# Moving 24 weight stores from ScalarE's queue to GpSimd's in an attention and MLP kernel

## The chip, the cores and the metric

The kernel runs on one core of one Trainium2 chip. The metric is the device time of one execution in microseconds (us). Unless another unit is given, all times below are microseconds, and times inside an execution count from the start of the profiled span.

## The reference, cut to what matters

Two kinds of layer alternate over an activation `x` of 2048 rows by 640 columns, in float32: attention over a dilated sliding window (32 heads of 20, a window of 8 keys at a distance of 2), then an MLP (640 to 1536 to 640, GELU), then both once more with the same weights. Each is preceded by a layer norm and added to `x`.

```
x = x + A(layernorm(x), wqkv, wo)          # q, k, v = x @ wqkv; window softmax; @ wo
x = x + B(layernorm(x), w1, b1, w2, b2)    # layernorm(x); gelu(x @ w1 + b1) @ w2 + b2
x = x + A(layernorm(x), wqkv, wo)
x = x + B(layernorm(x), w1, b1, w2, b2)
```

## The kernel before, in words

**Precision.** Every float32 matmul is made of three float16 ones. An operand is split into a high half and a low half; high by high, high by low and low by high are added up in PSUM. Weights are scaled by 64 first.

**Units.** The 2048 rows are cut into four units of 512 rows (4 tiles of 128). One layer of one unit is a block `n` or `b` from 0 to 7; blocks 0 to 3 are the first layer, 4 to 7 the second. A block goes through: a layer norm; the qkv product on TensorE (L522), drained from PSUM by ScalarE (`ev`, L537) and spilled to memory by a DMA that ScalarE issues (L543); windows of q, k and v fetched back by SyncE's queue (L562); the window attention on VectorE (L601 to L639); the output product (L667); a second layer norm; the MLP, whose first product (L721) goes through GELU on ScalarE (L727, L730) and a subtraction on VectorE (L732) into the second product (L742). Three PSUM tiles (`ps`) serve L522, L667 and L721 in turn, so TensorE stops when ScalarE or VectorE leaves three of them undrained.

**The MLP weights.** `w1` and `w2` don't stay on chip. They are split once, early on, and written to memory as float16 pairs (`mw`); each pass of the MLP reads them back (L714, 216 loads over the whole kernel). The splitting runs in 24 steps (12 slices of 128 hidden columns, for `w1` and `w2` each), named `prep_m`:

1. SyncE's queue loads 320 KB of float32 weights into a staging slot (L382; 8 steps at first, blocks of `wo` among them, through four slots in `yT`, the rest through four slots `sa` in the tile `act`).
2. ScalarE writes the high half into a slot of `c1` or `c2` (L356).
3. VectorE writes the low half beside it (L357), which frees the staging slot.
4. A DMA stores the pair (320 KB) to `mw` (L397). Its landing frees the slot of `c1` or `c2`; there are three of each.

The same six slots take the weights that the MLP reads back later. The first product of the MLP waits until all low halves are written (`split_done`).

**The order of work.** Nothing is scheduled on the chip: each engine runs its own program in order, and an instruction whose semaphore hasn't come holds up all that stand behind it on that engine. The order is written when the kernel is built, by the class `Plan`. Each operation has an engine, a duration, a priority and what it needs; `Plan.run` plays the engines forward with these durations, always takes the operation that can begin first (among those that can, the one of the lowest priority number), and sorts all operations by the start that comes out. For a DMA it also keeps `hw`, until when the last DMA's issue lasts (on whichever engine), and `bus`, until when the queued bytes take; a DMA marked `lazy`, as the stores to `mw` are, isn't started earlier than 3 us before the bus is free. So a duration in the plan doesn't slow the chip, but it decides the order in which every engine's program is written.

**GpSimd.** Its other work is a few constants at the start, eight small operations for the first two layer norms (L449) and 30 operations that raise a variance to the power of -0.5 (L471). ScalarE makes the variance (L468) and waits for the result (L475).

The step that changes, and the helper that gives a DMA its cost in the plan:

Of the kernel before, what the change touches and what calls it, by code (L numbers as in the profile page):

```python
# [40 lines left out]
AHEAD = 1.5  # L41

ENDS = 2

HURRY = {3: 0.9, 7: 0.9, 11: 0.9}

# [157 lines left out]
def sliding_dilated_then_mlp_kernel(  # L204
# [18 lines left out]
    nc = tc.nc  # L223
# [11 lines left out]
    plan = Plan(SLOTS)  # L235
# [29 lines left out]
    def tile_of(pool, key):  # L265
        return T[pool][plan.slot[pool, key]]
# [20 lines left out]
    mw = [[dram.tile([P, 2, D], HT, name=f"mw{i}{f}") for f in range(NF)] for i in range(2)]  # L287
# [15 lines left out]

    def dma(kb, prio, emit, need=(), give=(), use=(), by="sp"):
        lazy = give[0][0] in ("x", "sq", "st", "c1", "c2", "zero", "mw") or give[0] in ("b1", "b2")
        plan.add(by, 0.1 if by == "act" else 0.38, prio, emit, need, give, use, move=kb / 330.0, lazy=lazy)

    def dma_transpose(prio, emit, need=(), give=(), use=()):
        plan.add("sp", 1.45, prio, emit, need, give, use, move=1.4)
# [16 lines left out]
    def identity():  # L326
# [4 lines left out]
    pool(0.3, -850, mask_index, give=["mi"])  # L331
    dve(32, -850, mask_value, need=["mi"], give=["mask"])
    dma(6, 40, lambda: nc.sync.dma_start(b1, bass.AP(tensor=B_b1.tensor, offset=B_b1.offset, ap=[[1, P], [P, NF]])),
        give=["b1"])
    dma(320, 41, lambda: nc.sync.dma_start(b2, bass.AP(tensor=B_b2.tensor, offset=B_b2.offset, ap=[[0, P], [1, D]])),
        give=["b2"])

    zk = ("sa", "zero")
    pool(0.3, -840, lambda: nc.gpsimd.memset(tile_of(*zk)[:HALO, :GC], 0.0), give=["zeros"], use=[zk])
    for la in range(2):  # L340
        for par in range(2):
            def clear(la=la, par=par):
                to = spill[la][par]
                z = tile_of(*zk)[:HALO, :GC]
                nc.sync.dma_start(bass.AP(tensor=to.tensor, offset=to.offset, ap=[[GC, HALO], [ROWS * GC, 3 * NG], [1, GC]]),
                                  z[:, None, :].to_broadcast([HALO, 3 * NG, GC]))

            dma(54, -490 + 300 * la + 100 * par, clear, need=["zeros"], give=[("zero", la, par)], use=[zk])
# [27 lines left out]
    def prep_rows(name, prio, src, hi, lo, use=()):  # L376
        key = (through[name], name)

        def load():
            st = tile_of(*key)  # L380
            w = src()
            nc.sync.dma_start(st.rearrange("p (k c) -> p k c", k=w.shape[1]) if len(w.shape) == 3 else st, w)  # L382

        dma(P * D * 4 / 1e3, prio, load, need=[("ev", 0, M - 1, 0)], give=[("st", name)], use=[key])
        a, v = split(hi, lo, lambda: tile_of(*key))
        act(D, prio, a, need=[("st", name)], give=[("hi", name)], use=[key, *use])
        dve(D, LOP[key[0]], v, need=[("hi", name)], give=[("lo", name)], use=[key, *use])
# [4 lines left out]
    def prep_m(f, i, prio):  # L392
        ck = (f"c{i + 1}", ("prep", f))
        src = (lambda: B_w2[f * P:(f + 1) * P]) if i else (
            lambda: B_w1.rearrange("(k p) c -> p k c", p=P)[:, :, f * P:(f + 1) * P])
        prep_rows(("m", f, i), prio, src, lambda: tile_of(*ck)[:, 0], lambda: tile_of(*ck)[:, 1], [ck])
        dma(328, prio - 5, lambda: nc.scalar.dma_start(mw[i][f], tile_of(*ck)),  # L397
            need=[("lo", ("m", f, i))], give=[("mw", f, i)], use=[ck], by="act")

    def turn(prio, t, name, key, yk):  # L400

# [280 lines left out]
    def mlp(at, b, t0, t1):  # L682
# [12 lines left out]
        tiles = range(t0, t1)  # L695
        ends = ENDS if at == len(PARTS) - 1 else 1
        closing = []
# [113 lines left out]
    for f in range(NF):  # L811
        for i in range(2):
            prep_m(f, i, 10 + f)
# [49 lines left out]
```

## Time and profile before

| | us |
|---|---|
| median of 3 runs (lowest, highest) | 1173.69 (1172.49, 1174.92) |
| the profiled execution, own time | 1173.78 |
| its span, first to last instruction | 1171.8 |
| TensorE busy | 1156.6 |
| VectorE busy | 1017.9 |
| ScalarE busy | 513.5 |
| GpSimd busy | 50.6 |

The span is what the trace covers; the profiled execution's own time is 1.98 us longer. Busy time of TensorE is the time in which at least one matmul is in flight. Its mean granted clock is 0.998 of full speed.

### The profile page before, as it was taken

To read this page: it belongs to the slowest core of one execution; us is meant where nothing else is said; L and a number is where in the kernel's file an instruction comes from. 1 tells how busy PE (TensorE), PEld (TensorE's weight loads), DVE (VectorE), ACT (ScalarE), POOL (GpSimd) and SP (SyncE) were. 2 spreads that over 40 slices of the span, in tenths; PEclk is the share of its full clock that TensorE was granted. 3 is DMA by queue.
4 is the path that set the end of the run, shared out by engine and by line. 5 is a ranking of instruction groups with operands and counts; after the bars stand their busy time and mean duration, and the time that the engine had idled before them with its cause. 6 is when DMAs were issued, how large, how long until landed. Compare 5 with 4: busy or idle time off the path is not lost.

```text
span 1171.8 us, 17254 instructions
## 1 busy us (share of the span) xinstructions
PE 1156.6 (99%) x6902; PEld 626.4 (53%) x6902; DVE 1017.9 (87%) x989; ACT 513.5 (44%) x925; POOL 50.6 (4%) x46
## 2 busy tenths in 40 slices
PE   8999999999999999999999999999999999999998
PEld 5444445577655455444655465545555655565554
DVE  8898999999899999999999999999999999821211
ACT  5385345446355336723446334373423453343211
POOL 1010002000000001100101000000100000000000
PEclk9999999999999999999999999999999999999999
DMA  9989999887987475775675666568655774545432
GB/s 304 331 294 247 270 329 284 241 270 247 219 219 213 154 206 145 206 191 173 169 208 176 175 194 191 179 170 189 180 191 180 208 196 134 177 102 135 146 102 79
DMA packets 219773, 235.01 MB, mean 201 GB/s; under 512 B 129884, under 2 KB 170412, under 8 KB 219692
## 3 DMA queue, kind: packets, MB, share of 16 engines
q1 hardware_dynamic: 190636, 194.57, 59.6%
q10 hardware_dynamic: 29056, 39.33, 10.0%
q8 instruction: 54, 0.88, 0.3%
q14 instruction: 27, 0.22, 0.1%
HBM read 158.93 MB, written 44.78 MB: 174 GB/s over the span
## 4 chain that ended last, share of the span: by engine, by line
PE 84%; DMA 7%; DVE 6%; issue 2%; ACT 1%; SPq 0%; POOL 0%; ACTq 0%; DVEq 0%
PE ps L522 29%; PE ps L721 22%; PE acc L742 22%; PE ps L667 11%; DMA yT<-hl 3%; DMA act<-in_B_w_dram 2%; DVE pr L601 1%; DVE sm L605 1%; DVE pr L627 1%; DVE pr L635 1%; DMA qk<-spill 1%; DVE act L732 1%; DMA pr<-in_A_wqkv_dram 0%; DVE xf L777 0%; DMA mw<-c 0%
## 5 line engine op out<-in xcount | busy, mean ns | idle before, releaser
L522 PE MATMUL ps<-wq,yT 128*128 128x480 f16 x1920 | 391.7, 366 | 4.2 <-ACT ev L537 2.8
L742 PE MATMUL acc<-c,act 128*128 128x512 f16 (+1 forms) x2310 | 330.4, 299 | 0.5 <-DVE xf L777 0.5
L721 PE MATMUL ps<-yT,c 128*128 128x512 f16 (+1 forms) x1620 | 328.2, 355 | 2.2 <-issue 1.4
L522 PEld LDWEIGHTS <-yT 128*128 128x128 f16 x1920 | 187.4, 98 | 205.6 <-issue 4.0
L742 PEld LDWEIGHTS <-act 128*128 128x128 f16 x2310 | 181.6, 98 | 141.9 <-DVE act L732 0.2
L721 PEld LDWEIGHTS <-c 128*128 128x128 f16 x1620 | 154.4, 98 | 148.9 <-issue 2.9
L727 ACT ACTIVATE act<-ps,b 128x512 f32<-128x512 f32 (+1 forms) x108 | 68.9, 639 | 299.2 <-PE ps L721 289.4
L601 DVE TENSOR_TENSOR pr<-qk 128x2560 f32<-128x2560 f32 x64 | 179.6, 2807 | 2.5 <-DMA qk<-spill 2.5
L627 DVE TENSOR_TENSOR pr<-sm,v 128x2560 f32<-128x2560 f32 x64 | 179.3, 2818 | 0.3
L605 DVE TENSOR_REDUCE sm<-pr 128x128 f32<-128x2560 f32 x64 | 179.2, 2800 | 0.0
L732 DVE TENSOR_TENSOR act<-act 128x512 f16<-128x512 f32 (+1 forms) x108 | 67.2, 626 | 94.3 <-ACT act L730 93.8
L635 DVE TENSOR_TENSOR pr<-pr 128x1280 f32<-128x1280 f32 (+1 forms) x128 | 143.9, 1149 | 0.2
L537 ACT ACTIVATE ev<-ps 128x480 f32<-128x480 f32 x128 | 72.1, 564 | 151.8 <-PE ps L522 141.3
L667 PE MATMUL ps<-wo,yT 128*128 128x320 f16 x960 | 133.4, 301 | 2.2 <-ACT ev L537 2.2
L667 PEld LDWEIGHTS <-yT 128*128 128x128 f16 x960 | 94.4, 98 | 41.1 <-DMA yT<-ohl 2.7
L471 POOL TENSOR_TENSOR ln<-ln,half 128x2 f32<-128x2 f32 (+1 forms) x30 | 44.9, 1496 | 976.3 <-ACT ln L468 976.3
L454 ACT ACTIVATE junk<-xf 128x640 f16<-128x640 f32 x56 | 41.2, 735 | 68.4 <-DVE xf L673 59.9
L730 ACT ACTIVATE act<-act 128x512 f16<-128x512 f32 (+1 forms) x108 | 62.4, 580 | 2.6
L493 DVE TENSOR_TENSOR hl<-y,hl 128x640 f16<-128x640 f32 x60 | 48.2, 818 | 8.0 <-ACT hl L491 7.9
L485 ACT ACTIVATE y<-xf,ln 128x640 f32<-128x640 f32 x56 | 49.4, 911 | 10.0 <-DVE hl L493 9.1
L491 ACT ACTIVATE hl<-y 128x640 f16<-128x640 f32 x60 | 42.9, 727 | 21.5 <-DMA yT<-hl 19.4
L458 ACT ACTIVATE junk<-xf,ln 128x640 f16<-128x640 f32 x56 | 46.1, 823 | 0.9
(53 smaller groups left out, 462.9 us busy)
## 6 DMA issues: line engine op xcount, KB each, us to landing
c<-mw SPq DMA_DIRECT2D x216, 320.0 KB, 3.2
spill<-ev ACTq DMA_DIRECT2D x64, 480.0 KB, 4.5
qk<-spill SPq DMA_DIRECT2D x32, 880.0 KB, 6.7
v<-spill SPq DMA_DIRECT2D x32, 880.0 KB, 5.1
qk<-spill SPq DMA_DIRECT2D x32, 320.0 KB, 3.7
mw<-c ACTq DMA_DIRECT2D x24, 320.0 KB, 6.2
act<-in_B_w_dram SPq DMA_DIRECT2D x21, 320.0 KB, 6.7
xf<-in_A_x_dram SPq DMA_DIRECT2D x16, 320.0 KB, 6.0
```

The costliest lines, as they stand in the source:

```text
L522: nc.tensor.matmul(ps, transposed(yk)[:, a * KD + k, t * P:(t + 1) * P], wq[:, b, k, g], start=first and j == 0, stop=last and j == len(to ...
L537: act(3 * GC, -400 + n, lambda i=i, pk=pk, ek=ek: nc.scalar.activation(tile_of(*ek)[:, :, i], tile_of(*pk)[:, :3 * GC].rearrange("p (a c) ...
L601: nc.vector.tensor_mul(tile_of(*pk), w[:, HALO + m + t0:HALO + m + t0 + EH, None, :].to_broadcast([P, EH, W, GC]), windows(w, t0, [GC, W], ...
L605: dve(E, G - 0.7, lambda pk=pk, t0=t0: nc.vector.tensor_reduce(lg(t0, t0 + EH).rearrange("p t w h -> p (t w h)"), tile_of(*pk).rearrange(" ...
L627: nc.vector.tensor_mul(tile_of(*vk).rearrange("p t w (h d) -> p t (w h) d", d=DH), lg(t0, t0 + EH).rearrange("p t w h -> p t (w h)")[:, :, ...
L635: dve(EH * w * GC, G - 0.9, lambda vk=vk, w=w: nc.vector.tensor_add(tile_of(*vk)[:, :, 0:w], tile_of(*vk)[:, :, 0:w], tile_of(*vk)[:, :, w ...
L667: nc.tensor.matmul(tile_of(*pk)[:, :D // 2], transposed(yk)[:, a * KD + k, t * P:(t + 1) * P], wo[:, b, k, c * D // 2:(c + 1) * D // 2], s ...
L721: nc.tensor.matmul(tile_of(*pk)[:, :nt], tile_of(*ck)[:, a, k * P:(k + 1) * P], transposed(yk)[:, c * KD + k, t0 * P:t1 * P], start=i == 0 ...
L727: act(nt, -430, lambda pk=pk, h32=h32, e=e: nc.scalar.activation(tile_of(*h32)[:, :nt], tile_of(*pk)[:, :nt], AF.Gelu_apprx_tanh, bias=b1[ ...
L730: act(nt, -440, lambda h32=h32, hk=hk: nc.scalar.activation(tile_of(*hk)[:, 0, :nt], tile_of(*h32)[:, :nt], AF.Copy), need=[("h", j)], giv ...
L732: dve(nt, -1000, lambda h32=h32, hk=hk: nc.vector.tensor_sub(tile_of(*hk)[:, 1, :nt], tile_of(*h32)[:, :nt], tile_of(*hk)[:, 0, :nt]), nee ...
L742: nc.tensor.matmul(accs[k][:, c0:c0 + n], tile_of(*hk)[:, a, (i - t0) * P:(i - t0 + 1) * P], tile_of(*wk)[:, c, w0:w0 + n], start=first, s ...
```

## The change

The 24 stores of `mw` are issued by GpSimd instead of ScalarE. In the plan they stand on GpSimd with an issue of 1.0 us, where they stood on ScalarE with 0.1 us. Loads and stores on the other queues keep their figures (0.38 us on SyncE's, 0.1 us on ScalarE's). Nothing else in the source changes; since the plan is played forward with other durations, the written order of other work may come out differently.

```
+ISSUE = {"sp": 0.38, "act": 0.1, "pool": 1.0}
...
     def dma(kb, prio, emit, need=(), give=(), use=(), by="sp"):
         lazy = give[0][0] in ("x", "sq", "st", "c1", "c2", "zero", "mw") or give[0] in ("b1", "b2")
-        plan.add(by, 0.1 if by == "act" else 0.38, prio, emit, need, give, use, move=kb / 330.0, lazy=lazy)
+        plan.add(by, ISSUE[by], prio, emit, need, give, use, move=kb / 330.0, lazy=lazy)
...
-        dma(328, prio - 5, lambda: nc.scalar.dma_start(mw[i][f], tile_of(*ck)),
-            need=[("lo", ("m", f, i))], give=[("mw", f, i)], use=[ck], by="act")
+        dma(328, prio - 5, lambda: nc.gpsimd.dma_start(mw[i][f], tile_of(*ck)),
+            need=[("lo", ("m", f, i))], give=[("mw", f, i)], use=[ck], by="pool")
```

## Rows read from the trace of the kernel before

**Rows 1.** The page: engine, busy us (share of the span), instructions.
```profile
PE 1156.6 (99%) x6902; PEld 626.4 (53%) x6902; DVE 1017.9 (87%) x989; ACT 513.5 (44%) x925; POOL 50.6 (4%) x46
```
**Rows 2.** Timeline of PE: start, length, work, [idle before it and releaser].
```profile
148.60 24.46 PE L522 MATMUL ps<-wq,yT 128*128 128x480 f16 x120 [1.34 <-ACT ev L537]
174.55 3.20 PE L522 MATMUL ps<-wq,yT 128*128 128x480 f16 x15 [1.49 <-ACT ev L537]
179.99 18.15 PE L667 MATMUL ps<-wo,yT 128*128 128x320 f16 x120 [2.24 <-ACT ev L537]
...
348.54 3.40 PE L721 MATMUL ps<-yT,c 128*128 128x512 f16 x15 [0.73 <-DMA yT<-hl]
471.95 9.87 PE L721 MATMUL ps<-yT,c 128*128 128x512 f16 x45 [1.43 <-issue]
```
**Rows 3.** Windows: stretch, length, busy of PE, PEld, DVE, ACT, POOL; PEclk, DMA share, GB/s.
```profile
86.00:100.00 14.00, 14.00 (x71) 6.75 (x70) 14.00 (x13) 8.94 (x22) 1.14 (x2) 1.00 0.68 205
...
175.00:190.00 15.00, 12.76 (x76) 7.77 (x75) 13.98 (x14) 5.95 (x12) 1.02 (x1) 0.89 1.08 261
```
**Rows 4.** The chain that ended last: start us, us, what.
```profile
136.27 11.06 DMA act<-in_B_w_dram
...
165.78 7.50 DMA act<-in_B_w_dram
173.32 4.29 DMA mw<-c
...
308.15 16.30 PE ps L667 x120
```
**Rows 5.** Line L397 (the stores): ns min/median/max, first and last start; time to landing.
```profile
L397 ACTq DMA_DIRECT2D mw<-c x24: 326/339/1952, 86.2 to 206.4; - x24
...
DMA to landing us min/median/max: 3.3/6.2/12.1
```
**Rows 6.** Waits from 80 to 250 us: who waited for whom, us, times, longest.
```profile
ACT c L356 <- DMA act<-in_B_w_dram: 16.8, 7, 6.5
...
ACT ev L537 <- DVE c L357: 4.2, 2, 2.8
...
ACT ev L537 <- issue: 3.1, 2, 2.1
```
**Rows 7.** Timeline of ACT and its queue (ACTq).
```profile
125.61 0.33 ACTq L397 DMA_DIRECT2D mw<-c  x1
...
147.35 0.74 ACT L356 ACTIVATE c<-act 128x640 f16<-128x640 f32 x1 [6.51 <-DMA act<-in_B_w_dram]
...
173.31 0.74 ACT L356 ACTIVATE c<-act 128x640 f16<-128x640 f32 x1 [1.78 <-DMA act<-in_B_w_dram]
173.32 0.34 ACTq L397 DMA_DIRECT2D mw<-c  x1
...
177.69 0.74 ACT L356 ACTIVATE c<-act 128x640 f16<-128x640 f32 x1 [0.85 <-DMA mw<-c]
...
205.13 0.29 ACT L475 ACTIVATE ln<-ln 128x1 f32<-128x1 f32 x1 [3.26 <-POOL ln L471]
```
**Rows 8.** Windows of line L357 alone (low halves): stretch, length, DVE busy (instructions).
```profile
40.00:97.00 57.00, 6.14 (x8) 1.00 0.90 282
97.00:135.00 38.00, 3.28 (x4) 1.00 1.12 280
```
**Rows 9.** DMA issues from 135 to 148 us: KB each, median us to landing.
```profile
mw<-c ACTq DMA_DIRECT2D x4, 320.0 KB, 12.0
```
**Rows 10.** Line L382 (weight loads): time from issue to landing.
```profile
DMA to landing us min/median/max: 4.2/6.4/11.1
```
**Rows 11.** Timeline of DVE: the low halves of one stretch.
```profile
164.94 3.02 DVE L357 SCALAR_TENSOR_TENSOR c<-act,c 128x640 f16<-128x640 f32 x4
```
**Rows 12.** Line L471 on POOL: ns min/median/max, starts; and two of them in the timeline.
```profile
L471 POOL TENSOR_TENSOR ln<-ln,half x30: 543/1022/5322, 67.6 to 1052.9; 128x2 f32<-128x2 f32 x26, 128x1 f32<-128x1 f32 x4
...
199.78 5.84 POOL L471 TENSOR_TENSOR ln<-ln,half 128x1 f32<-128x1 f32 x2 [6.08 <-ACT ln L468]
```

## The prediction

> **What bounds the kernel now.** I read the page's busy times first. TensorE has a matmul in flight for 1156.6 of 1171.8 us, VectorE is busy for 1017.9, ScalarE for 513.5, GpSimd for 50.6 [rows 1]. So the kernel lasts as long as TensorE's work plus TensorE's pauses, and the pauses are 1171.8 - 1156.6 = 15.2 us. A change that leaves the matmuls alone can give back some of these 15.2 us, or add to them.
>
> Next, TensorE's own timeline, to see where the pauses lie [rows 2]. Three of them, 1.34, 1.49 and 2.24 us, lie between 147 and 180 us, inside the stretch in which the weights are split and stored (86.2 to 206.4 us [rows 5]): 5.07 us together. After 200 us only small ones follow, of which the two largest are 0.73 and 1.43 us. The rest of the 15.2 lies ahead of 20 us and behind the last matmul, out of this change's reach. A second loss goes with the third pause: between 175 and 190 us the granted clock is 0.89 [rows 3], below the upper level of 2.4 GHz, right behind TensorE's two pauses of 1.49 and 2.24 us; the 120 matmuls of the output product take 18.15 us there [rows 2] and 16.30 us at the full clock [rows 4], a difference of 1.85 us. So what a perfect splitting stretch could return is 5.07 + 1.85 = 6.92 us.
>
> Then ScalarE's waits in that stretch, because all three pauses end at a drain by ScalarE (`ev`, L537) [rows 2]. The reader is to see that most of its waiting is for weight loads (16.8 us in 7 waits); waits that stand around the stores, for a low half (4.2 us) or for no visible reason (3.1 us), come to 7.3 us [rows 6]. Pause by pause, from ScalarE's timeline and the chain:
>
> - The first pause. ScalarE stood 6.51 us at a high half, until 147.35, for a load [rows 7] that had been issued at 136.27 and took 11.06 us to land [rows 4], where the median of these loads is 6.4 [rows 10]. The drains stood behind it.
> - The second. The same at 173.31 (1.78 us) [rows 7], for a load that took 7.50 us [rows 4].
> - The third. At 177.69 a high half waited 0.85 us for a store to land, to get its slot of `c` [rows 7]. That store was issued at 173.32 and took 4.29 us [rows 4]; it stood in ScalarE's program behind the high half of 173.31.
>
> **The change part by part.** *The issue leaves ScalarE.* 24 issues of 0.339 us (median) are 8.1 us of its queue [rows 5]. ScalarE is idle for more than half of the span [rows 1], and TensorE is covered by three PSUM tiles: a qkv tile of 15 matmuls takes 24.46 / 8 = 3.06 us [rows 2], so a drain may be about 6.1 us late. Cost or gain of the issue as such: 0. Without that cover each would count its 0.34 us, 8.1 us in all.
>
> *The low half no longer holds up ScalarE.* A store waits for its low half, and everything behind it on ScalarE waits too; these are the 7.3 us above. None of the three pauses ends at such a wait, so I take 0; the bounds are 0 and, if one of them merely fed a later pause, that pause, which is counted below.
>
> *The stores leave earlier.* On ScalarE a store goes when its place in the program comes. Up to 135 us, 12 low halves have been written [rows 8], one of them of `wo` and 11 of the stored weights; the seventh store goes at 125.61 [rows 7], so four stores lag. They go out together between 135 and 141 us and take 12.0 us to land [rows 9], beside the load of 136.27 with its 11.06. GpSimd has next to nothing ahead of them, so they would leave soon after their low halves, partly into the stretch from 86 to 100 us, where the DMA engines are 0.68 busy [rows 3]. If the load then lands in its median 6.4 us, ScalarE goes on 4.7 us earlier, and the first pause (1.34) is gone. For the third pause, the store of 173.32 can follow the low halves that are ready by 164.94 + 3.02 = 167.96 [rows 11], 5.4 us sooner, and the high half at 177.69 doesn't wait: -0.85 of the 2.24. The second pause can go either way. Its load, issued at 165.78, would share the DMA engines with up to three further stores. A megabyte takes 1 / 0.261 = 3.8 us at the 261 GB/s of a full stretch [rows 3], so three stores of 0.33 MB cost up to 3.8 us more, and at best the pause vanishes (-1.49). I take 0, as stores that have left earlier also empty the queue.
>
> *The clock.* If the third pause shrinks to 1.39 us and the first is gone, the 1.85 us of slower matmuls may come back wholly or not at all. I take the middle, -0.9.
>
> *GpSimd's side.* No row shows a DMA issue on this engine. The nearest below is the issue on ScalarE's queue, 0.33 us (minimum) [rows 5]; the nearest on the engine itself are its 30 small operations, 0.54 to 5.32 us, median 1.02 [rows 12]. I take 1.02, the row of the same engine: 24 x 1.02 = 24.5 us on an engine that is idle for 1121. Behind a store that waits stand only those powers (L471), and behind a power ScalarE's L475. The place where it can hurt is the second layer norm of block 0: two powers take 5.84 us from 199.78 [rows 12], and ScalarE waits 3.26 us for them until 205.13 [rows 7]. One store ahead of them adds 1.02, at most 5.32. 3.26 + 1.02 = 4.3 is inside the 6.1 us of cover, so 0; at 5.32 it is 8.6, and TensorE would pause 2.5 us.
>
> *SyncE's queue* issues the loads as before. It loses and gains no instruction, but its order, as that of all engines, comes from the plan. There the issue takes 1.0 instead of 0.1, which pushes other DMAs back by up to 0.9 us for each of 24 stores. I take 0 for the forecast and price it as a rival.
>
> The sum: -1.34 - 0.85 + 0 - 0.9 = -3.1 us against the profiled execution's own 1173.78 (its span of 1171.8 and 1.98 around it, which I leave as it is): 1170.7. The median of the runs, 1173.69, is 0.09 lower, so 1170.6. At best 1173.7 - 6.9 = 1166.8.
>
> **The rivals.** *Hidden anyway.* ScalarE is rid of 24 instructions, but the pauses are waits for loads, and these take what they take. For it: two of the three pauses are waits for loads, and 16.8 us of ScalarE's waits. Against it: the loads were late beside four stores that had piled up. Time: 1173.7, within 2.3. The Trainium skill (DMA: Bandwidth & Descriptors, section "Issuing engines are not separate DMA queues") speaks for this rival: transfers started from any engine share the same 16 DMA engines, and issuing from several saves only the sequencer's time to start them. By that rule alone the gain would be that of the issues, which are hidden, and the time 1173.7; the rows agree that the issue is short (0.339 us) and don't show whether an earlier start helps.
>
> *A new order, slower.* The plan is played with other figures from the first store on, so the drains of all later blocks can be written in another place. One drain behind a load or a transpose that comes more than the 6.1 us of cover late makes a pause such as the three here: 1.3 to 2.2 us, with the clock's loss 3.2 to 4.1. From 200 us on, there is almost nothing to win (the largest pauses are 0.73 and 1.43 us) and 970 us in which to lose. Against it: a shift of at most 0.9 us per store is small beside that cover. One such pause with the clock's loss beyond what the stretch gives back: 1177 to 1178; three: 1186. It decides where ScalarE is held for more than 6.1 us.
>
> *GpSimd is late.* Its operations stretch to 5.32 us, when VectorE is nearly always busy. If each store leaves 5.32 - 1.02 = 4.3 us later than I take it, slots of `c` come free later, high halves wait, drains stand behind them: one place like that of 177.69 gives +4.3 (1178), and, as 24 steps through 6 slots reuse them three times, at most 12.9 (1186.6). It decides from 5.4 us after the low half, since the store of 173.32 is that late already; that speaks against it. The Trainium skill (SBUF — State Buffer, section "SBUF: two separate sides", the box on VectorE blocking DMA) says that GpSimd writes the descriptors of its DMAs itself, and can't while VectorE is in a mode that takes both ports. By that rule a store would wait out VectorE's long operations and the time would be this rival's; the section "Who interferes with whom" leaves two-operand operations and reductions, which the long ones here are, outside these modes. Whether descriptors are held up, no row shows.
>
> **How the numbers follow.** This measurement can tell about 0.2%, 2.35 us, from no change. Forecast (faster, 1170.6, its own range 1166.8 to 1171.3): 0.38. Hidden: 0.27. New order: 0.22. GpSimd late: 0.13. So faster 0.38, same 0.27, slower 0.35. For the range I go down to 1166.8, all that the stretch can return, and up to 1181, which takes in one new pause or one late place and a second one's share; two and more such places, some 0.12, stay above, and some 0.04 below.
>
> **What would show it.** In the profile after, 24 issues of `mw` from POOL's queue and none from ScalarE's. Right: they follow their low halves by 1 to 3 us; the loads around 136 to 148 us land in less than 11 us; TensorE's pauses between 140 and 190 us sum to about 3 instead of 5.07, with a clock near 1.0 from 175 to 190; after 200 us the pauses stay near 2.5 us. Wrong by the second rival: new pauses after 200 us, or drains behind other instructions than before. Wrong by the third: stores that leave over 5 us behind their low halves, and high halves that wait for stores. Wrong by the first: the waits for loads unchanged.

## The result, and the profile after

Over 22 executions of each kernel the median went from 1173.77 to 1176.94, a ratio of 1.0034 with a 95% interval of 1.0022 to 1.0047: the change made the kernel slower, by 0.34%. The forecast was 1170.6 and faster. Two later comparisons, told below, gave 1.0002 (0.998 to 1.0023) and 1.0019 (0.9996 to 1.0042), which both take in 1. So the loss is small and clear in the first comparison alone, but nothing points to the gain.

The profiled execution after took 1172.4, with a span of 1170.5; it is the fastest of the 22, so its span can't be set against that of before. What it shows is where the pauses lie. First the page, busy time by engine.

```profile
span 1170.5 us, 17283 instructions
...
PE 1154.9 (99%) x6902; PEld 625.5 (53%) x6902; DVE 1017.5 (87%) x989; ACT 513.2 (44%) x925; POOL 61.8 (5%) x70
```

The work is the same as in [rows 1]; GpSimd has 24 more instructions and 11.2 us more. Next TensorE's timeline (start, length, work, idle before it and releaser); lines of the code stand two lower than before, so L522, L537 and L667 are now L524, L539 and L669.

```profile
109.77 6.24 PE L524 MATMUL ps<-wq,yT 128*128 128x480 f16 x30 [2.02 <-ACT ev L539]
117.08 12.31 PE L524 MATMUL ps<-wq,yT 128*128 128x480 f16 x60 [1.07 <-ACT ev L539]
129.81 48.76 PE L524 MATMUL ps<-wq,yT 128*128 128x480 f16 x240 [0.42 <-ACT ev L539]
180.19 4.25 PE L669 MATMUL ps<-wo,yT 128*128 128x320 f16 x30 [1.62 <-DMA yT<-ohl]
...
237.10 1.26 PE L744 MATMUL acc<-c,act 128*128 128x512 f16 x8 [0.25 <-DVE act L734]
...
470.91 9.87 PE L723 MATMUL ps<-yT,c 128*128 128x512 f16 x45 [0.99 <-issue]
```

The first two pauses of [rows 2], at 148.60 and 174.55, are gone; the forecast had the first one gone and the second as it was. Three new ones stand at 109.77, 117.08 and 129.81, 3.51 us together, in a stretch where the trace of before has 0.14 us, and each ends at a drain. The third old pause has become one of 1.62 that ends at a transpose (`yT<-ohl`). After 200 us the longest pause is 0.99, where it was 1.43.

So the question is what held up the drains before 130 us. ScalarE's timeline tells it.

```profile
99.28 0.37 ACTq L545 DMA_DIRECT2D spill<-ev  x1
108.53 0.74 ACT L493 ACTIVATE hl<-y 128x640 f16<-128x640 f32 x1 [9.28 <-DMA yT<-hl]
109.17 0.55 ACT L539 ACTIVATE ev<-ps 128x480 f32<-128x480 f32 x1
```

ScalarE stands for 9.28 us in front of a half of the layer norm's output (`hl`, L493), because its buffer is still being read by a DMA transpose (`yT<-hl`) of SyncE's queue. The drain of 109.17 stands behind it, and TensorE starts again at 109.77. The two queues beside it, SyncE's and then GpSimd's:

```profile
95.39 12.42 SPq L497 DMA_TRANSPOSE yT<-hl  x2
```

```profile
95.41 0.58 POOL L399 DMA_DIRECT2D mw<-c  x1 [0.45 <-DVE c L359]
96.15 0.54 POOL L399 DMA_DIRECT2D mw<-c  x1 [0.16 <-issue]
...
98.35 0.54 POOL L399 DMA_DIRECT2D mw<-c  x1 [0.19 <-issue]
```

Five stores of 320 KB leave within 3 us, at the very time when SyncE issues two transposes, and the transposes keep its queue busy for 12.42 us. In the trace of before the same two stood like this, and the stores like the rows under it (SyncE's queue, then ScalarE's):

```profile
93.59 7.82 SPq L495 DMA_TRANSPOSE yT<-hl  x2
```

```profile
95.22 2.38 ACTq L397 DMA_DIRECT2D mw<-c  x2
...
105.94 0.33 ACTq L397 DMA_DIRECT2D mw<-c  x1
...
117.77 1.33 ACTq L397 DMA_DIRECT2D mw<-c  x2
```

What waited for them there, on ScalarE:

```profile
104.30 0.74 ACT L491 ACTIVATE hl<-y 128x640 f16<-128x640 f32 x1 [5.48 <-DMA yT<-hl]
```

On ScalarE two stores went beside the transposes and the others 10 and 22 us later, each at its place among the drains; the next is the 125.61 of [rows 7]. In the written order of after these stores are spread as well. But GpSimd's program has next to nothing between them, so nothing on the chip keeps them apart: each leaves as soon as its low half is written. The chain that ended last (start, us, what) says the same: beside [rows 4], the load of 136.27 with its 11.06 us is replaced by one of 7.75, and a transpose has entered.

```profile
95.39 13.12 DMA yT<-hl
...
140.66 7.75 DMA act<-in_B_w_dram
```

Last the stores' own row, for the forecast's price of GpSimd (ns min/median/max; then time to landing).

```profile
L399 POOL DMA_DIRECT2D mw<-c x24: 542/542/723, 54.3 to 206.6; - x24
...
DMA to landing us min/median/max: 2.5/5.9/8.7
```

An issue takes 0.54 us, half of the 1.02 taken, and one follows the other after 0.73; the stores land about as soon as from ScalarE (median 5.9 against 6.2 [rows 5]; in the two later profiles of each kernel 5.7 and 6.1 against 5.6 and 5.9). GpSimd is not late.

### The profile page after: what moved, and what is told of

It is laid out like the page before. It is cut to its first block, busy times and chain, and to the rows that moved or that the text cites. A ratio compares the mean times of both kernels' runs of the same rounds, so it can differ in the third digit from the quotient of the medians.

```text
span 1170.5 us, 17283 instructions
## 1 busy us (share of the span) xinstructions
PE 1154.9 (99%) x6902; PEld 625.5 (53%) x6902; DVE 1017.5 (87%) x989; ACT 513.2 (44%) x925; POOL 61.8 (5%) x70
## 3 DMA queue, kind: packets, MB, share of 16 engines
q0 software_dynamic: 1920, 7.87, 1.7%
## 4 chain that ended last, share of the span: by engine, by line
PE 76%; DVE 12%; DMA 7%; issue 2%; ACT 2%; SPq 1%; POOL 0%; ACTq 0%; DVEq 0%
PE acc L744 24%; PE ps L723 24%; PE ps L524 18%; PE ps L669 10%; DMA yT<-hl 3%; DVE pr L603 2%; DVE pr L629 2%; DVE sm L607 2%; DMA act<-in_B_w_dram 1%; DVE pr L637 1%; DVE c L359 1%; DMA spill<-ev 1%; DMA yT<-in_A_wo_dram 1%; ACT c L358 1%; DMA pr<-in_A_wqkv_dram 1%
## 5 line engine op out<-in xcount | busy, mean ns | idle before, releaser
L524 PE MATMUL ps<-wq,yT 128*128 128x480 f16 x1920 | 391.6, 366 | 5.2 <-ACT ev L539 3.5
L524 PEld LDWEIGHTS <-yT 128*128 128x128 f16 x1920 | 187.4, 98 | 206.5 <-issue 4.3
L669 PE MATMUL ps<-wo,yT 128*128 128x320 f16 x960 | 132.1, 299 | 2.6 <-DMA yT<-ohl 2.1
L539 ACT ACTIVATE ev<-ps 128x480 f32<-128x480 f32 x128 | 72.0, 564 | 139.5 <-PE ps L524 137.4
L669 PEld LDWEIGHTS <-yT 128*128 128x128 f16 x960 | 93.7, 98 | 40.8 <-DMA yT<-ohl 2.9
L493 ACT ACTIVATE hl<-y 128x640 f16<-128x640 f32 x60 | 43.0, 727 | 23.6 <-DMA yT<-hl 21.5
```

The source lines that it names most:

```text
L524: nc.tensor.matmul(ps, transposed(yk)[:, a * KD + k, t * P:(t + 1) * P], wq[:, b, k, g], start=first and j == 0, stop=last and j == len(to ...
L539: act(3 * GC, -400 + n, lambda i=i, pk=pk, ek=ek: nc.scalar.activation(tile_of(*ek)[:, :, i], tile_of(*pk)[:, :3 * GC].rearrange("p (a c) ...
L669: nc.tensor.matmul(tile_of(*pk)[:, :D // 2], transposed(yk)[:, a * KD + k, t * P:(t + 1) * P], wo[:, b, k, c * D // 2:(c + 1) * D // 2], s ...
```

## The experiments

The theory after the first reading: **the burst**. ScalarE's program had paced the stores; without that pace five run beside two transposes, `hl` waits, drains wait, TensorE pauses. The rivals: **the order**, that the rewritten order of other work makes the loss (it differs between 59 and 220 us, from 59 us on SyncE's queue and from 87 us on ScalarE and VectorE; TensorE's never does); **the engine**, that a DMA from GpSimd is dearer whenever it leaves; and **chance**, that the executions vary more than the change.

The numbers of all runs stand in one table. Ratios are against the kernel before on the same chip, with 95% intervals; behind a median stand 22 executions for the first two rows, 10 to 12 for the others, 7 for `burst_only` and 4 for `after_twice`. The transposes are the two that SyncE issues near 95 us (the row of its queue); the last three columns are TensorE's idle time in the profiled execution, as the length of the window less its busy time.

| run | median (before) | ratio (interval) | transposes | 90-135 | 135-175 | 175-200 |
|---|---|---|---|---|---|---|
| before, as shown above | 1173.77 | | 7.82 | 0.14 | 2.83 | 2.24 |
| after | 1176.94 (1173.77) | 1.0034 (1.0022, 1.0047) | 12.42 | 3.51 | 0 | 2.61 |
| after_again | 1175.77 (1174.46) | 1.0002 (0.998, 1.0023) | 12.45 | 1.67 | 0.43 | 4.56 |
| queue_alone | 1179.88 (1174.46) | 1.0032 (1.0013, 1.0052) | 11.80 | 1.89 | 1.82 | 5.89 |
| order_alone | 1175.57 (1174.46) | 1.001 (0.9989, 1.0031) | 7.13 | 0 | 0.28 | 2.28 |
| queue_paced | 1177.25 (1174.46) | 1.0019 (0.9993, 1.0044) | 7.76 | 0 | 2.60 | 1.34 |
| after_held | 1173.03 (1173.84) | 0.9988 (0.9968, 1.0007) | 7.09 | 0 | 0.22 | 3.42 |
| act_early | 1175.45 (1173.84) | 1.0008 (0.9989, 1.0026) | 9.12 | 6.46 | 0 | 0.50 |
| after_twice | 1204.61 (1173.84) | 1.0262 (1.0218, 1.0305) | 9.28 | 0 | 8.88 | 4.78 |
| after_third | 1177.0 (1174.55) | 1.0019 (0.9996, 1.0042) | 12.54 | 3.90 | 0 | 3.13 |
| held_again | 1176.66 (1174.55) | 1.0012 (0.999, 1.0034) | 7.87 | 1.34 | 1.74 | 2.33 |
| held_first | 1180.46 (1174.55) | 1.0056 (1.0028, 1.0085) | 8.18 | 1.04 | 14.88 | 2.08 |
| queue_held | 1182.57 (1174.55) | 1.0069 (1.0047, 1.0091) | 6.38 | 5.85 | 3.33 | 1.36 |
| burst_only | 1181.24 (1172.8) | 1.0069 (1.004, 1.0098) | 15.13 | 5.24 | 0.22 | 2.14 |
| rest_only | 1174.24 (1172.8) | 1.0003 (0.9983, 1.0023) | 8.82 | 1.09 | 1.91 | 5.36 |
| before_2 (one execution, 1176.87) | | | 8.40 | 1.60 | 1.98 | 4.97 |
| before_3 (one execution, 1174.34) | | | 7.78 | 0.21 | 2.34 | 2.14 |

### The parts of the change apart

`after_again` repeats the kernel after. `queue_alone` takes the kernel before, with its order, and only lets GpSimd issue the stores; `order_alone` takes the order of after and lets ScalarE issue them. `queue_paced` is `queue_alone` with a small copy on GpSimd ahead of each store, which reads a column of the drain that stands last before the store in ScalarE's program, so that the store leaves about when it left before.

The edit of `queue_alone` on the kernel before (that of `order_alone` on the kernel after is the same line, back again):

```diff
-        dma(328, prio - 5, lambda: nc.scalar.dma_start(mw[i][f], tile_of(*ck)),
+        dma(328, prio - 5, lambda: nc.gpsimd.dma_start(mw[i][f], tile_of(*ck)),
             need=[("lo", ("m", f, i))], give=[("mw", f, i)], use=[ck], by="act")
```

And of `queue_paced`, where each drain sets `latest[0]` to a column of its own when it is written into the program:

```diff
+        def store():
+            nc.gpsimd.tensor_copy(pace, latest[0])
+            nc.gpsimd.dma_start(mw[i][f], tile_of(*ck))
...
-        dma(328, prio - 5, lambda: nc.scalar.dma_start(mw[i][f], tile_of(*ck)),
+        dma(328, prio - 5, store,
```

What was expected:

> The changed kernel once more, for a second profile of it, since the first one (1172.4 us, span 1170.5) is the fastest of 22 runs with a median of 1176.9. All theories: 1172 to 1180. Pile-up theory: five stores that GpSimd issues between 95 and 99 us lie beside two DMA transposes that SyncE issues at 95.4, TensorE pauses between 107 and 130 us by 3 us or more, and a run near 1177 shows longer pauses there or a clock below 1.0 behind them. Order theory: in a run near 1177 the additional pauses lie elsewhere, at instructions whose place in the written order has changed.

> GpSimd issues the 24 stores, but the plan still counts them as ScalarE's with 0.1 us, so every other instruction keeps its order of before. Pile-up theory (stores freed from ScalarE's program leave in a burst behind their low halves and slow the transposes on SyncE's queue): 1176 to 1179, pauses between 95 and 130 us. Order theory (the slowdown comes from the new written order): 1173.8 within 1.2. Theory that a DMA issued by GpSimd is by itself late: 1176 to 1180, with high halves that wait for stores.

> The plan counts the stores as GpSimd's with 1.0 us, so the order is that of the changed kernel, but ScalarE issues them, each at its place in that order. Pile-up theory: 1173.8 within 1.2, no burst at 95 us. Order theory: 1176 to 1178, pauses where the changed kernel has them. GpSimd-late theory: 1173.8 within 1.2.

> As queue_alone, and ahead of each store GpSimd copies one column of the drain that ScalarE wrote last before the store's place, so that the store leaves no earlier than on ScalarE; 24 small copies are added. Pile-up theory: 1173.8 within 1.5, no burst at 95 us. Order theory: the same, as the order is that of before. GpSimd-late theory: 1176 to 1180.

The queue alone is as slow as the whole change (1.0032, interval above 1), and the order alone can't be told from before (1.001), though the two intervals overlap. In `queue_alone` the stores leave at 93.02 (two), 94.48, 95.21, 95.95 and 96.69, and the transposes beside them take 11.80; with the order of after and ScalarE's queue they take 7.13. With the pace put back they take 7.76 though GpSimd issues the stores. The rows, of SyncE's queue in `queue_alone`, `order_alone` and `queue_paced`:

```profile
93.48 11.80 SPq L495 DMA_TRANSPOSE yT<-hl  x2
```

```profile
93.65 7.13 SPq L497 DMA_TRANSPOSE yT<-hl  x2
```

```profile
94.01 7.76 SPq L501 DMA_TRANSPOSE yT<-hl  x2
```

So the length of the transposes goes with when the stores leave, and not with the order. The time of `queue_paced`, 1.0019, lies between, and its interval takes in both; it is 2.8 us above before, where the burst's theory allowed 1.5. `after_again` measured no loss at all, and its pauses before 135 us are 1.67 where 3 or more were expected, but its profile shows the same 12.45 us of transposes; it weakens the size.

TensorE's pauses follow less simply. In `queue_alone` ScalarE waits 6.80 us for `hl`, little more than the 6.1 us of cover, and the pauses before 135 us are 1.89, hardly more than the 1.60 of `before_2`; the longest, 4.04, stands ahead of the output product. So where the 5.4 us that its median lost lie isn't shown. And the first two pauses of before are still in its timeline, though all its stores leave early:

```profile
151.31 24.46 PE L522 MATMUL ps<-wq,yT 128*128 128x480 f16 x120 [1.82 <-ACT ev L537]
177.62 3.20 PE L522 MATMUL ps<-wq,yT 128*128 128x480 f16 x15 [1.86 <-ACT ev L537]
```

In `order_alone`, where ScalarE still paces the stores, neither is there (0.28 from 135 to 175). As far as one profile of each can tell, early stores alone don't take these pauses away.

### Holding the burst, or making it elsewhere

`after_held` is the kernel after with a copy on GpSimd ahead of each store that reads the last transpose written ahead of it, so that a store starts behind that transpose. `act_early` is the kernel before with six stores put right behind their low halves in ScalarE's program. `after_twice` issues each store twice, for twice the traffic.

`after_held` has the `store` of `queue_paced`, with `latest[0]` set by each transpose:

```diff
+            def flip(t=t, hk=hk):
+                nc.sync.dma_start_transpose(
+                    transposed(yk)[:, :, t * P:(t + 1) * P], tile_of(*hk).rearrange("p a b -> p (a b)"))
+                latest[0] = transposed(yk)[:, 0, t * P:t * P + 1]
```

`act_early`, in the step that writes a low half; `EARLY` holds (0,1), (1,0), (1,1), (2,0), (2,1) and (3,0), and these six have no store elsewhere:

```diff
+            low()
+            if name[0] == "m" and name[1:] in EARLY:
+                f, i = name[1:]
+                nc.scalar.dma_start(mw[i][f], tile_of(*use[0]))
```

`after_twice`:

```diff
-        dma(328, prio - 5, lambda: nc.gpsimd.dma_start(mw[i][f], tile_of(*ck)),
+        dma(328, prio - 5, lambda: [nc.gpsimd.dma_start(mw[i][f], tile_of(*ck)) for _ in range(2)],
```

> The changed kernel, and ahead of each store GpSimd copies one column of the tile that the last transpose written ahead of the store made, so that no store passes a transpose that stands before it in the plan; 24 small copies are added. Pile-up theory: the two transposes that SyncE issues at 94 us take 7 to 8 us instead of 12.4, TensorE pauses less than 0.5 us between 100 and 130 us, 1172.5 to 1175.5. Theory that GpSimd's queue is slower by itself, whenever a store leaves: transposes near 12, 1176 to 1179.

> The kernel before, stores on ScalarE's queue, but the second to the seventh store stand in ScalarE's program right behind their own low halves instead of at the places of the plan, so that six stores leave between 92 and 98 us on a hardware queue. Pile-up theory: the transposes at 94 us take 11 us or more, TensorE pauses 1 to 4 us between 100 and 130 us, 1176 to 1179. Theory that only GpSimd's queue does it: transposes 7 to 8 us, 1173 to 1176.

> The changed kernel with each of the 24 stores issued twice by GpSimd, with the same bytes. Pile-up theory: transposes at 94 us take 15 us or more, pauses of TensorE between 100 and 130 us of 5 us or more, 1180 to 1190. Theory that the slowdown is the presence of GpSimd's queue or the new order: within 2 of the changed kernel, 1174 to 1179.

`after_held` did what the burst's theory asks: the transposes take 7.09, the pauses before 175 us are gone but for 0.22, and the median is 0.8 below that of before; its interval still holds 1. Its repeat below is less kind.

`act_early` is mixed. With early stores on ScalarE's queue, four within 2.4 us at 93.65, 94.39, 95.12 and 96.05 and a fifth at 99.81, the transposes take 9.12, more than 7.82 and less than 12.42, and between the two theories' forecasts; ScalarE stands for 10.11 us:

```profile
107.36 1.03 ACT L547 ACTIVATE ev<-ps 128x480 f32<-128x480 f32 x2 [10.11 <-DMA mw<-c]
```

TensorE pauses 6.46 us there. The profile puts the wait down to a store's landing; the chain that ended last has the transposes there, 11.94 us from 94.38, and which of the two it was isn't settled. Early stores can hurt from ScalarE's queue too, then, but the time is 1.0008, and no pause is left from 135 to 175 us. TensorE comes to that stretch 6.46 us later, which alone may hide the pauses there.

`after_twice` failed as a test of dose. The second store of a pair waits until the first has landed, so the five never run at once and the transposes take 9.28. What it prices is another thing, the forecast's third rival. Its waits from 140 to 235 us (who waited for whom, us, times, longest):

```profile
POOL mw L399 <- DMA mw<-c: 76.1, 15, 9.2
...
ACT c L358 <- DMA mw<-c: 26.0, 5, 8.8
...
ACT ln L477 <- POOL ln L473: 17.0, 2, 16.6
```

A GpSimd that does stand in front of its stores makes slots of `c` late (26.0 us of ScalarE) and keeps a power of the layer norm from ScalarE for 16.6 us at once: +2.6%. None of it is in the kernel after.

### Repeats, and how long to hold

`after_third` and `held_again` repeat. `held_first` holds the first eight stores alone, as below; `queue_held` puts the hold of `after_held` on `queue_alone`.

```diff
+            if f < 4:
+                nc.gpsimd.tensor_copy(pace, latest[0])
-            nc.gpsimd.tensor_copy(pace, latest[0])
```

> The changed kernel a third time, on the same chip as the next three. Pile-up theory and order theory alike: 1.5 to 4 us above the kernel before; in its profile the two transposes at 94 us take about 12 us and TensorE pauses 1.5 us or more between 100 and 130 us.

> after_held once more beside the changed kernel. Pile-up theory: 2 to 4 us below after_third, between -2.5 and +0.5 of the kernel before, transposes at 94 us in 7 to 8 us. If its first result was chance: as after_third.

> As after_held, but only the stores of the first four weight slices (8 of 24) wait for a transpose; the other 16 leave behind their low halves. Pile-up theory, if the burst at 95 us is what costs: as after_held within 1.5. If the later bursts (four stores at 162 to 165 us) cost as much: 1 to 2 us above after_held, pauses between 165 and 190 us.

> queue_alone (GpSimd issues, order of before), with each store held behind the last transpose written ahead of it. Pile-up theory: the 4 us that queue_alone lost come back, within 1.5 of the kernel before, transposes at 94 us in 7 to 8 us. If holding helps only with the new order: 1176 to 1179.

`after_third` shows the transposes at 12.54 and 3.90 us of pauses before 135, as the first profile did. `held_again` has no burst beside the transposes (7.87), but comes out at 1.0012 (0.999 to 1.0034): together with the first time, the held kernel is neither faster nor slower than before by anything that this measurement can tell. It is 0.3 us below `after_third`, where 2 to 4 were expected, so taking the burst away doesn't clearly give the loss back. In both held executions five stores leave in a group later, from 144.85 and from 148.36 us, within 3.4 us, and the pauses from 135 to 175 us (0.22 and 1.74) are no longer than those of before (1.98 to 2.83): a group as such doesn't show as a loss there.

The other two came out as losses, against the simple theory that any hold helps, and show what else counts. In `held_first` the stores leave in a group later: four from 135.72, beside a transpose issued at 134.18 that holds SyncE's queue for 8.26 us; the weight load behind it, issued at 142.50, takes 20.37 us, and ScalarE stands in front of its high half. From SyncE's queue, the chain, and ScalarE's timeline:

```profile
134.18 8.26 SPq L505 DMA_TRANSPOSE yT<-hl  x1
142.50 0.57 SPq L386 DMA_DIRECT2D act<-in_B_w_dram  x1
```

```profile
142.50 20.37 DMA act<-in_B_w_dram
```

```profile
162.95 0.74 ACT L360 ACTIVATE c<-act 128x640 f16<-128x640 f32 x1 [22.14 <-DMA act<-in_B_w_dram]
```

That is the same burst in another place, and a pause of 14.88 us in this execution, which took 1190.83 (the median is 1180.46). In `queue_held` the hold is too long: stores that left at 93 to 97 now leave from 110.07 on, their slots come free late, and the next high half waits for one. GpSimd's row, then ScalarE's:

```profile
110.07 0.58 POOL L400 DMA_DIRECT2D mw<-c  x1
```

```profile
117.05 0.74 ACT L358 ACTIVATE c<-act 128x640 f16<-128x640 f32 x1 [10.42 <-DMA mw<-c]
```

Both costs exist, then: too early and in a group, the transposes and the loads behind them are late; too late, the slots are.

### Which stores carry the loss

What was left open was whether the five stores beside the transposes make the loss, or the queue of all 24. `burst_only` keeps the order of after and lets GpSimd issue those five alone; `rest_only` lets it issue the other 19. The kernel before was profiled twice more, to see how its own pauses vary.

```diff
+FIVE = ((1, 0), (1, 1), (2, 0), (2, 1), (3, 0))
...
-        dma(328, prio - 5, lambda: nc.gpsimd.dma_start(mw[i][f], tile_of(*ck)),
+        dma(328, prio - 5, lambda: (nc.gpsimd if (f, i) in FIVE else nc.scalar).dma_start(mw[i][f], tile_of(*ck)),
```

> Order of the changed kernel; only the five stores that left together at 95 to 98 us are issued by GpSimd, the other 19 by ScalarE at their places in that order. Pile-up theory (these five beside the transposes cost the time): transposes at 94 us near 12 us, TensorE pauses 1.5 to 4 us between 100 and 130 us, 1.5 to 4 us slower than the kernel before. If the loss is spread over all bursts, or is GpSimd's queue in general: transposes 7 to 12, less than 1.5 us slower.

> The reverse: those five stores are issued by ScalarE at their places, the other 19 by GpSimd, order of the changed kernel. Pile-up theory: transposes at 94 us in 7 to 8 us, TensorE pauses less than 0.5 us between 100 and 130 us, within 1.5 us of the kernel before. If the later bursts cost as much: 1.5 to 4 us slower, pauses behind 130 us.

> The kernel before once more, for a second profile of its pauses. Pile-up theory: the two transposes at 93.6 us take 7 to 8.5 us, TensorE pauses less than 0.5 us between 100 and 130 us, and 2 to 6 us between 130 and 200 us.

> The kernel before, a third profile. As before_2. If the transposes vary between 7 and 12 us without any store moved, the theory falls.

The five alone cost 1.0069 (1.004 to 1.0098); the 19 others cost nothing that can be told, 1.0003 (0.9983 to 1.0023). The intervals don't meet, so a loss goes with these five. It is 8.4 us in the median, where 1.5 to 4 were expected, and more than all 24 together cost in any comparison: the parts don't add up, and why isn't known. The repeats of before show no burst, but `before_2` has 1.60 us of pauses before 135 all the same, where less than 0.5 was expected (`rest_only` has 1.09), so the kernel's own pauses vary by about 1.5 us there, as much as `after_again` shows in all. The transposes of `burst_only` and of `rest_only`, on SyncE's queue:

```profile
93.04 15.13 SPq L500 DMA_TRANSPOSE yT<-hl  x2
```

```profile
97.10 8.82 SPq L500 DMA_TRANSPOSE yT<-hl  x2
```

And in `burst_only` the whole way from there to TensorE. Its DMA issues from 92 to 106 us (KB each, median us to landing), its waits from 80 to 130 us, TensorE's timeline, and two windows (length; busy of PE, PEld, DVE, ACT, POOL; PEclk, DMA share, GB/s):

```profile
mw<-c POOLq DMA_DIRECT2D x5, 320.0 KB, 13.0
...
yT<-hl SPq DMA_TRANSPOSE x2, 17.6
```

```profile
ACT hl L496 <- DMA yT<-hl: 12.5, 1, 12.5
```

```profile
112.52 53.56 PE L527 MATMUL ps<-wq,yT 128*128 128x480 f16 x255 [5.25 <-ACT ev L542]
```

```profile
105.00:110.00 5.00, 2.27 (x12) 0.98 (x10) 0.00 (x0) 0.00 (x0) 0.00 (x0) 0.93 1.38 108
110.00:115.00 5.00, 2.48 (x7) 0.97 (x7) 2.96 (x3) 3.19 (x5) 0.00 (x0) 0.50 0.82 151
```

The transposes land after 17.6 us, `hl` waits 12.5, the pause is 5.25 (with 12.5 us of waiting and about 6.1 of cover, 6.4 was to be expected), and behind it, up to 115 us, the granted clock is 0.50, the lower level of 1.2 GHz.

## Why the prediction was wrong

**The step that failed** is the third part of the change, "The stores leave earlier", with its -1.34 and -0.85 and the -0.9 of the clock that hangs on them. The stores did leave earlier, but neither half of what followed was as forecast.

First, the loss. The prediction counted an early start as a gain only, because the stretch from 86 to 100 us has a DMA share of 0.68 [rows 3]; it did not ask which other transfers run there, who waits for them and how many stores would start together. [rows 8] has eight low halves by 97 us, when three stores had left. It should have gone through ScalarE's waits before 130 us as it did behind it: in the trace of before, `hl` already stands 5.48 us for the same transposes, with drains behind it, close to the 6.1 us of cover. In the profile after it stands 9.28 us, 3.2 over that cover, and TensorE pauses 3.51 us. The 7.82 and 12.42 say how long the transposes held SyncE's queue; `hl` came free 104.30 - 93.59 = 10.71 us behind their start in before and 108.53 - 95.39 = 13.14 after. So 2.4 us of the longer wait are longer transposes, and the other 1.4 are a ScalarE that reaches the wait sooner behind their start.

Second, the gain. ScalarE was to go on 4.7 us earlier at the first pause. Its high half starts at 148.50, where it was 147.35, and its waits from 80 to 250 us are still waits for loads:

```profile
148.50 0.74 ACT L358 ACTIVATE c<-act 128x640 f16<-128x640 f32 x1 [5.77 <-DMA act<-in_B_w_dram]
```

```profile
ACT c L358 <- DMA act<-in_B_w_dram: 18.6, 7, 5.8
```

In the three profiles of before the high halves wait 17.6, 16.4 and 16.4 us for DMAs in that stretch (loads, stores that keep a slot, once a spill), in those of after 18.6, 15.0 and 17.3 (loads alone). The waits for stores are gone, and about as much waiting for loads stands in their place.

The sizes, as means over the three profiles of before and the three of after in the table: idle time of TensorE from 90 to 135 us went from 0.65 to 3.03, a loss of 2.4; from 135 to 175 us from 2.38 to 0.14, a gain of 2.2; from 175 to 200 us from 3.12 to 3.43. From 90 to 175 us together it is 3.03 before and 3.17 after: the pauses stand further ahead, and none of the time is returned.

- *The first pause, -1.34.* It is gone, but not by the forecast's way. The load whose lateness made it takes 7.75 us instead of 11.06 (8.86 in `after_again`), not the 6.4 taken; ScalarE's wait in front of its high half is 5.77 instead of 6.51, just inside the cover; and TensorE comes there later by its new pauses. In `queue_alone` the same load takes 10.63 us and the pause is 1.82. That early stores took it away isn't shown.
- *The second, 0.* It is gone too, -1.49, better than forecast, but it is 1.86 in `queue_alone`.
- *The third, -0.85.* It did not come. 1.62 stands in its place in the first profile, behind a transpose instead of a store, and the mean from 175 to 200 us is 0.3 higher. The prediction had a wait here that doesn't decide: in the trace of before, TensorE's weight load for that product stands 2.7 us for the same transposes (its waits from 80 to 250 us, below), and in `before_2` and `before_3` the pause itself ends at them (3.46 and 2.13).

```profile
PEld L667 <- DMA yT<-ohl: 2.7, 1, 2.7
```

- *The clock, -0.9.* From 175 to 190 us it was 0.89, 0.77 and 0.89 in the profiles of before and 1.00, 0.89 and 1.00 in those of after; but in `after_third` it was 0.92 from 90 to 135, where it was 1.00 before. As a mean over a whole execution its median was 0.998 for both kernels in each of the two later comparisons, so there is no gain to count.
- *GpSimd's issue.* 0.54 against 1.02, and hidden: right, and with room to spare.
- *The issue off ScalarE, the low half.* At 0 both stand: the waits for a low half and for no visible reason, 7.3 us in before, are gone in the profile after, and no time came of it.

**The rivals.** *Hidden anyway* had the better of the gain: the pauses are waits for loads, and ScalarE waits for DMAs as long as before. It missed the loss. The rule behind it, of the Trainium skill (DMA: Bandwidth & Descriptors, section "Issuing engines are not separate DMA queues"), agrees with the runs in the part that I drew nothing from: stores from GpSimd's queue made transposes from SyncE's longer, 12.42 against 7.82, as on shared engines they would. *A new order* shows no loss: the order of TensorE's work is the same throughout and that of all others from 220 us on, and `order_alone` is 1.001 (0.9989 to 1.0031); it does move pauses, as seen above. *GpSimd is late* fell: its issues take 0.54 us, with VectorE busy for 87% of the span. The Trainium skill's box on VectorE blocking DMA (SBUF — State Buffer, section "SBUF: two separate sides") does not show in this trace: no issue took longer than 0.72. It was not put to the test either, because the long operations here are of the kinds that the prediction names as outside those modes.

The loss came by a way that no rival had: a burst on an empty queue. Nearest is the second, which priced a drain that stands behind a transpose for more than the 6.1 us of cover, but expected it from a new order. The prediction had put 0.35 on slower, and 1176.94 lies within its range of 1166.8 to 1181; that range was drawn for other causes, so this is luck.

**What stays open.** The way from the five stores to TensorE is shown in single profiles (11.80 to 15.13 us of transposes beside them, 6.4 to 9.3 in every other profile), and a loss in the time for these five alone. That the loss of the whole change goes this way is argued: of the kernels without the burst, `after_held` (0.9988) is below every comparison of after (1.0002 to 1.0034), but `held_again` (1.0012) and `queue_paced` (1.0019) are not. The pauses add up to +0.5 in the means (2.4 - 2.2 + 0.3), the medians of after are 1.3 to 3.2 above those of before, and the three profiled spans of each kernel differ by 0.5 as means (1173.6 against 1173.0). So where the rest of the median's loss lies, over the executions without a profile, isn't shown. And with stores early, the transposes took 9.12 from ScalarE's queue and 11.80 to 15.13 from GpSimd's: whether that is the queue, or the fifth store's later start in `act_early`, was not tried apart.

## What to carry to other kernels

A queue's place in a busy engine's program is also a throttle: before a DMA is moved to an idle engine, ask what had kept it from leaving, and what runs on the DMA engines at the moment when all that is ready leaves at once. Go through the waits that are still inside their cover, not only through those that already show as pauses, because these are the ones that a burst pushes over. Read a pause in a second profile before pricing it: behind the first pause of before stood a load, in `before_2` a store's landing (6.42 us); the third ended at a drain, in both repeats at the product's own transposes. If the stores must be kept apart on an idle queue, tie each to something that happens when it should leave: here a hold that was too long, or one that let a group go beside a transpose, cost more (1.0069 and 1.0056) than the whole change (1.0034), and no version tried is faster than the kernel before beyond what the measurement can tell.

## What the runs showed of the hardware

- Two DMA transposes held SyncE's queue for 7.1 to 8.8 us where ScalarE's program paced the five stores of 320 KB (before and its repeats, `order_alone`, `rest_only`), and for 11.8 to 15.1 us beside the same five from GpSimd's queue (after and its repeats, `burst_only`; six in `queue_alone`).
- GpSimd issued a store of 320 KB in 0.54 us, one every 0.73, and it landed in 5.9 us (median), about as from ScalarE's queue (6.2 [rows 5]).
- Behind a pause of 5.25 us on TensorE, in `burst_only`, the granted clock was 0.50 up to 115 us, for 2.5 us of matmuls; from 117 us on it was 1.00 again.
